# Attention and a gated feed-forward layer on one core: the normalisation is stated at the start of an attention step, and the first feed-forward units at the start of the last steps

## The chip, the cores and the metric

The kernel runs on one core of a Trainium2 chip. The metric is the device time of one execution, in microseconds (us); less is better. Before the change it is 1184.77 us, the median of 3 runs (1184.61 to 1186.2). The core has five engines, each with a queue of its own that it works through in order: TensorE (PE; its weight loads are shown apart as PEld), VectorE (DVE), ScalarE (ACT), GpSimd (POOL), and SyncE (SP), which here only issues DMA transfers.

## The reference

Attention with a forget gate over 8 batches of 8 heads, 576 positions and 64 dimensions, then a feed-forward layer (512 to 2048 to 512) over the 4608 tokens. Shapes and the handling of inputs are left out:

```python
def _attn_ref(q, k, v, f):
    scores = np.matmul(q, k.transpose(0, 1, 3, 2)) / np.sqrt(D)
    cum = np.cumsum(np.log(np.clip(f, 0.0001, 1.0)), axis=-1)
    decay = cum[:, :, :, None] - cum[:, :, None, :]
    scores = np.where(causal, -1000000000.0, scores + decay)
    attn = np.exp(scores - np.max(scores, axis=-1, keepdims=True))
    attn = attn / (np.sum(attn, axis=-1, keepdims=True) + 1e-09)
    return np.matmul(attn, v)

def _moe_ref(x, w_in, w_out):
    h = x @ w_in
    sp = np.maximum(h, 0.0) + np.log1p(np.exp(-np.abs(h)))
    return (h * erf(sp)) @ w_out
```

`causal` marks the keys behind a query. The inputs are float32, the weights float64.

## The kernel before

**Two phases.** Attention runs in 64 steps, two for each pair of heads, followed by four steps in which the last tiles drain while the feed-forward layer begins. Then the feed-forward layer runs alone. A step's tile holds some of the query blocks of both heads: an even step the blocks of 576 and 192 keys, an odd step those of 448, 320 and 64 keys (`BLOCKS`, `END`). A tile t passes through these stages, each in a step of its own as far as the loop `for t in range(NH + 5)` puts it there:

- step t: `scores(t)` on TensorE (L358, then a matmul that adds the mask, L363), into a PSUM pool `ps_s` of two buffers, one for each head, which is used again in the next step; `reduce(t, 0)` and `reduce(t, 1)` on VectorE (L379) add the decay, write the row to SBUF as `pr` and accumulate its extreme into `st`.
- step t + 1: `exps` on ScalarE (L391), for one head and then the other, with the row sums accumulated into `st`.
- step t + 2: `normalize`, which adds 1e-9 to the sums and takes their reciprocal on VectorE (L396, L397) and multiplies the rows of `pr` by it on GpSimd (L401).
- step t + 3: `transposes` on TensorE (L413) into three PSUM banks `t`, four for an odd tile, of which only three buffers exist, so that the fourth waits until the first is evacuated; `evacuate` copies the banks to SBUF as `pt`, the first two on ScalarE (L422), the others on VectorE (L420, L418).
- step t + 4: `values` on TensorE (L440), into the one buffer of `ps_o`.
- step t + 5: `store`, copies on VectorE (L449, L452, L453) to `xo`, and after an odd step a DMA to `xt_d` (L455).

**Order.** TensorE, VectorE, ScalarE and GpSimd run their instructions in the order in which the code states them. Only SP's DMAs are ordered by a scheduler. What one step states for an engine is therefore a queue: before the change VectorE has `store`, two `reduce`, `evacuate`, the reciprocal, and last a piece of `convert`.

**Weights on the side.** From step 4 to step 67 each step also has one piece of `convert`, which turns float64 weights into two float32 parts: for each of 16 loads one piece on ScalarE (L285), then one on VectorE (L289), then two instructions (L294, L296), then two (L299, L302) and one on GpSimd (L303).

**Feed-forward.** A unit (256 tokens by 256 of the 2048 features) is one `Moe.step`: `up` has 24 matmuls (L126) into a PSUM tile `ph`; ScalarE computes softplus (L132) into `e`; in groups of units the error function follows (L135), each change of function with a table load; VectorE multiplies and rounds (`gate`, L141 and L143), GpSimd takes the rest (L144), and `down` comes at least four units later (L163 to L165). A step that loads the next x also casts it on ScalarE (L111) and subtracts on GpSimd (L112). The first four units, of the first 256 tokens, are stated in steps 64 to 67. Their PSUM is that of `ps_s`, which is free after step 63. `up` of unit 0 to 3 therefore stands at the end of TensorE's part of these steps, behind `transposes` and `values`.

Of the kernel before, what the change touches and what calls it, by code (L numbers as in the profile page):

```python
# [225 lines left out]
def attention_moe(ctx, tc, q2, k2, vp, f, w_in, w_out, out):  # L226
# [32 lines left out]
    moe = Moe(tc, xt_d, out, xp, wide4)  # L259
# [51 lines left out]
    with ExitStack() as ph:  # L311
# [18 lines left out]
        def load(p):  # L330

            q = io.tile([P, PAD + S], F32, name=f"q{p}", tag="q")
            k = io.tile([P, S], F32, name=f"k{p}", tag="k")
            nc.sync.dma_start(out=q, in_=q2[p // NP, p % NP])
            nc.sync.dma_start(out=k, in_=k2[p // NP, p % NP])
            c = io.tile([P, 2, S], F32, name=f"c{p}", tag="c")
            if p:
                for j in range(2):
                    n = 2 * p + j
                    nc.sync.dma_start(out=c[:, j], in_=cum_d[n:n + 1].rearrange("a s -> (a s)").partition_broadcast(P))  # L340
            pairs[p] = [q, k, c]

        def load_values(p):

            v = wk.tile([P, 9, P], F32, name=f"v{p}", tag="v")
            nc.sync.dma_start(out=v, in_=vp[p // NP, p % NP].rearrange("p (c d) -> p c d", c=9))
            vals[p] = v

        def scores(t):


            p, half = divmod(t, 2)
            q, k = pairs[p][:2]
            s = [ps_s.tile([P, 1024], F32, name=f"s{t}_{j}", tag="s") for j in range(2)]
            for at, i, k0, k1 in PARTS[half]:
                for j in range(2):
                    h = slice(64 * j, 64 * j + 64)
                    nc.tensor.matmul(out=s[j][:, at:at + k1 - k0], lhsT=q[h, PAD + START[i]:PAD + END[i]],  # L358
                                     rhs=k[h, k0:k1], start=i > 0, stop=k1 < END[i])
            for j in range(2):  # L360
                for i in BLOCKS[half]:
                    first = max(0, START[i])
                    nc.tensor.matmul(out=s[j][:, SCOL[i] + first:SCOL[i] + END[i]], lhsT=eye,  # L363
                                     rhs=upper[:, first - START[i]:], start=False, stop=i != 3)
            raw_scores[t] = s
            probs[t] = wk.tile([P, TCOLS[half]], F32, name=f"pr{t}", tag=f"pr{half}")
            stats[t] = wk.tile([P, 3, 2, len(BLOCKS[half])], F32, name=f"st{t}", tag=f"st{half}")

        def row(t, i, j):

            return probs[t][:, TOFF[i] + j * END[i]:TOFF[i] + (j + 1) * END[i]]

        def reduce(t, j):
            p, half = divmod(t, 2)
            c, s, st = pairs[p][2], raw_scores[t][j], stats[t]
            for m, i in enumerate(BLOCKS[half]):
                to, score, decay_ = (x.rearrange("p (k n) -> p k n", n=64) for x in (
                    row(t, i, j), s[:, SCOL[i]:SCOL[i] + END[i]], c[:, j, :END[i]]))
                nc.vector.tensor_tensor_reduce(  # L379
                    out=to[:, ::-1] if j else to, in0=score, in1=decay_, scale=-0.125, scalar=BIG,  # L380
                    op0=ALU.add, op1=ALU.min, accum_out=st[:, 0, j, m:m + 1])
            if j:
                del raw_scores[t]
                if half:
                    del pairs[p]

        def exps(t, j):
            st = stats[t]
            for m, i in enumerate(BLOCKS[t % 2]):
                seg = row(t, i, j)  # L390
                nc.scalar.activation(out=seg, in_=seg, func=AF.Exp, bias=st[:, 0, j, m:m + 1], scale=-1.0,  # L391
                                     accum_out=st[:, 1, j, m:m + 1])

        def normalize(t):
            st = stats.pop(t)
            nc.vector.tensor_scalar(out=st[:, 1], in0=st[:, 1], scalar1=1e-9, scalar2=None, op0=ALU.add)  # L396
            nc.vector.reciprocal(out=st[:, 2], in_=st[:, 1])  # L397
            for m, i in enumerate(BLOCKS[t % 2]):
                for j in range(2):
                    seg = row(t, i, j)  # L400
                    nc.gpsimd.tensor_scalar(out=seg, in0=seg, scalar1=st[:, 2, j, m:m + 1], scalar2=1.0,  # L401
                                            op0=ALU.mult, op1=ALU.mult)

        def transposes(t, a):

            half = t % 2
            if a == 0:
                pts[t] = wk.tile([P, 1600 if half else 1536], F32, name=f"pt{t}", tag=f"pt{half}")
            banks[t, a] = b = ps_t.tile([P, 512], F32, name=f"t{t}_{a}", tag="t")
            for n, (i, j, *ch) in enumerate(BANKS[half][a]):  # L410

                at = TOFF[i] + (i * P if j is None else 2 * END[i] - ch[0] * P - P if j else ch[0] * P)
                nc.tensor.transpose(out=b[:, n * P:(n + 1) * P], in_=probs[t][:, at:at + P], identity=ident)  # L413

        def evacuate(t, a):
            b, pt = banks.pop((t, a)), pts[t]
            if a == 3:
                nc.vector.tensor_copy(out=pt[:, 1536:], in_=b[:, 64:128])  # L418
            elif a == 2:
                nc.vector.tensor_copy(out=pt[:, 1024:1536], in_=b)  # L420
            else:
                nc.scalar.copy(out=pt[:, 512 * a:512 * a + 512], in_=b)  # L422
            if a == len(BANKS[t % 2]) - 1:
                del probs[t]
# [18 lines left out]
        def store(t):  # L443
            p, half = divmod(t, 2)
            o = held.pop(t)
            if half == 0:
                held["x"] = xo = wk.tile([P, S], F32, name=f"xo{p}", tag="xo")
                blocks = xo[:, 64:].rearrange("p (a q) -> p a q", a=4)
                nc.vector.tensor_copy(out=blocks[:, ::3], in_=o[:, :256].rearrange("p (a q) -> p a q", a=2))  # L449
            else:  # L450
                xo = held.pop("x")
                nc.vector.tensor_copy(out=xo[:, 192:448], in_=o[:, :256])  # L452
                nc.vector.tensor_copy(out=xo[:, :64], in_=o[:, 256:320])  # L453
                b, pp = divmod(p, NP)
                nc.sync.dma_start(out=xt_d[pp * P:(pp + 1) * P, b * S:(b + 1) * S], in_=xo)  # L455
                del vals[p]

        NH = B * H
# [17 lines left out]
        for t in range(NH + 5):  # L476
            there = [0 <= t - n < NH for n in range(6)]
            p, half = divmod(t, 2)
            if half == 0 and t + 4 < NH:
                load(p + 2)  # L480
            if half == 0 and there[2]:
                load_values(p - 1)
            if there[5]:
                store(t - 5)
            if there[0]:
                scores(t)
            if there[1]:
                exps(t - 1, 0)
            if there[0]:
                reduce(t, 0)  # L490
            if there[3]:
                for a in range(3):
                    transposes(t - 3, a)
                evacuate(t - 3, 0)
            if there[3] and len(BANKS[(t - 3) % 2]) == 4:
                transposes(t - 3, 3)
            if there[4]:
                values(t - 4)
            if there[1]:
                exps(t - 1, 1)  # L500
            if there[0]:
                reduce(t, 1)
            if there[3]:
                for a in range(1, len(BANKS[(t - 3) % 2])):
                    evacuate(t - 3, a)
            if there[2]:
                normalize(t - 2)
            if t >= 4 and todo:
                convert(*todo.pop(0))
            if t == NH - 2:  # L510
                moe.load_x(0)
                moe.split_x(0)
            if t == NH - 1:
                early.close()
                moe.ep = moe_pools.enter_context(tc.tile_pool(name="ep", bufs=2, side="right"))
                moe.ps_ha = moe_pools.enter_context(tc.tile_pool(name="ps_ha", bufs=4, space=PSUM, side="right"))
            if NH <= t < NH + 4:
                moe.step()
        assert not todo and not pts and not held and not vals

    w2 = ctx.enter_context(tc.tile_pool(name="w2", bufs=1))
# [44 lines left out]
```

## Time and profile before

| | before |
|---|---|
| median of 3 runs | 1184.77 us |
| the profiled execution | 1185.39 us |
| its span, first to last instruction | 1183.6 us |
| attention, last start of scores (L358) | 342.29 us |
| start of feed-forward unit 0 (L126) | 354.42 us |
| first `down` (L163) | 377.92 us |
| mean granted TensorE clock | 0.999 |

Times in the profile count from the first instruction. In a row of the timeline the columns are start, duration, engine, line, operation, output and inputs by the program's names, and count; an idle time of the engine just before stands in brackets with what ended it. Rows of one kind that follow one another are merged. The two instructions of a matmul, its weight load (PEld) and the matmul (PE), are shown apart. A row of the chain of waits is a piece of time on the path that ended last, charged to the engine that worked in it. The profiled execution lasts 1.8 us longer than its span, for what lies around the first and the last instruction.

### The profile page before, as it was taken

What the parts mean: (1) busy time and instruction counts of PE and PEld (TensorE: products, weight loads), DVE (VectorE), ACT (ScalarE), POOL (GpSimd) and SP (SyncE); (2) the same over time, 40 slices, a digit from 0 to 9 for tenths busy, and PEclk for the clock granted to TensorE, in tenths of its full rate; (3) what the DMA queues carried; (4) which work ended last, traced back from release to release, by engine and by line L of the source; (5) the groups of instructions that cost most, each with busy time, mean ns of one, the idle gap of its engine ahead of it and who ended that gap; (6) DMA issues with size and microseconds to landing.
All of it is one profiled execution on the core that took longest, in us unless ns stands there. A gap on an engine that the chain in (4) does not pass through costs nothing.

```text
span 1183.6 us, 22838 instructions
## 1 busy us (share of the span) xinstructions
PE 1152.4 (97%) x8992; PEld 1010.0 (85%) x8992; DVE 563.4 (48%) x1473; ACT 598.9 (51%) x1231; POOL 474.1 (40%) x531
## 2 busy tenths in 40 slices
PE   5999999999999999999999999999999999999998
PEld 3777777777779999999999999998999999998987
DVE  4888888888874665665322322321231231231221
ACT  3777777777775676565423422432432342242432
POOL 1565666555673444444432432232232232232221
PEclk9999999999999999999999999999999999999999
DMA  7566767667641222421221221210110110100000
GB/s 249 187 229 230 240 215 244 213 220 239 208 145 56 79 100 75 139 73 54 89 72 54 77 85 54 71 37 1 37 36 1 36 35 2 37 15 23 18 19 18
DMA packets 56618, 118.68 MB, mean 100 GB/s; under 512 B 4672, under 2 KB 19008, under 8 KB 56512
## 3 DMA queue, kind: packets, MB, share of 16 engines
q1 hardware_dynamic: 56512, 117.23, 30.2%
q8 instruction: 71, 1.16, 0.4%
q14 instruction: 35, 0.29, 0.1%
HBM read 93.47 MB, written 23.74 MB: 99 GB/s over the span
## 4 chain that ended last, share of the span: by engine, by line
PE 82%; DVE 9%; POOL 7%; issue 1%; ACT 1%; DMA 0%; POOLq 0%; ACTq 0%
PE ph L126 35%; PE y L165 11%; PE y L163 11%; PE y L164 11%; POOL pr L401 7%; DVE pr L379 6%; PE s L358 5%; PE o L440 4%; PE t L413 3%; DVE pt L420 2%; PE s L363 1%; DVE st L397 1%; DMA fd<-in_f_dram 0%; DVE c L325 0%; DVE st L396 0%
## 5 line engine op out<-in xcount | busy, mean ns | idle before, releaser
L126 PE MATMUL ph<-xh,w 128*128 128x256 f32 x2304 | 435.8, 282 | 0.0
L126 PEld LDWEIGHTS ph<-xh,w 128*128 128x128 f32 x2304 | 367.0, 191 | 5.9
L144 POOL TENSOR_TENSOR gl<-e,gh 128x512 fp32r<-128x512 f32 x144 | 186.8, 1297 | 354.0 <-DVE gh L143 348.7
L126 PE MATMUL ph<-xl,w 128*128 128x256 f32 x1152 | 325.0, 282 | 0.0
L132 ACT ACTIVATE e<-ph 128x512 f32<-128x512 f32 x144 | 86.2, 598 | 448.3 <-PE ph L126 447.9
L401 POOL TENSOR_SCALAR pr<-pr,st 128x576 f32<-128x576 f32 (+4 forms) x320 | 179.9, 580 | 160.6 <-DVE st L397 132.7
L165 PE MATMUL y<-w,gl 128*128 128x512 f32 x576 | 228.2, 396 | 0.0
L163 PE MATMUL y<-w,gh 128*128 128x512 f32 x576 | 228.1, 396 | 0.0
L164 PE MATMUL y<-w,gh 128*128 128x512 f32 x576 | 227.2, 394 | 0.0
L126 PEld LDWEIGHTS ph<-xl,w 128*128 128x128 f32 x1152 | 219.3, 190 | 5.7
L391 ACT ACTIVATE pr<-pr,st 128x576 f32<-128x576 f32 (+3 forms) x320 | 176.5, 555 | 8.4 <-DVE st L379 8.4
L143 DVE CAST gh<-e 128x512 fp32r<-128x512 f32 x144 | 86.6, 601 | 174.6 <-PE y L164 163.0
L379 DVE CUSTOM_DVE_ANT_0 pr<-s,c 128x576 f32<-128x576 f32 (+3 forms) x320 | 136.5, 485 | 54.4 <-PE s L363 46.3
L141 DVE TENSOR_TENSOR e<-e,ph 128x512 f32<-128x512 f32 x144 | 97.9, 680 | 103.1 <-ACT e L135 101.7
L165 PEld LDWEIGHTS y<-w,gl 128*128 128x128 f32 x576 | 108.7, 189 | 25.9
L358 PE MATMUL s<-k,q 64*128 64x320 f32 (+4 forms) x768 | 114.8, 424 | 13.4 <-DMA k<-in_k_dram 8.3
L164 PEld LDWEIGHTS y<-w,gh 128*128 128x128 f32 x576 | 108.8, 189 | 20.7
L413 PE MATMUL t<-ident,pr 128*128 128x128 f32 x800 | 112.5, 281 | 14.0 <-POOL pr L401 12.9
L112 POOL TENSOR_TENSOR xl<-xr,xh 128x1024 fp32r<-128x1024 f32 x27 | 65.8, 2439 | 149.3 <-ACT xh L111 149.3
L163 PEld LDWEIGHTS y<-w,gh 128*128 128x128 f32 x576 | 108.8, 189 | 19.7
L422 ACT COPY pt<-t 128x512 f32<-128x512 f32 x128 | 73.6, 577 | 82.0 <-PE t L413 82.0
L358 PEld LDWEIGHTS s<-k,q 64*128 64x128 f32 x768 | 75.4, 194 | 43.4 <-issue 18.7
(50 smaller groups left out, 1009.3 us busy)
## 6 DMA issues: line engine op xcount, KB each, us to landing
v<-in_vp_dram SPq DMA_DIRECT2D x32, 576.0 KB, 6.1
c<-cum_d SPq DMA_DIRECT2D x62, 288.0 KB, 4.8
xr<-xt_d SPq DMA_DIRECT2D x27, 512.0 KB, 4.1
q<-in_q_dram SPq DMA_DIRECT2D x32, 320.0 KB, 2.9
k<-in_k_dram SPq DMA_DIRECT2D x32, 288.0 KB, 3.4
xt_d<-xo SPq DMA_DIRECT2D x32, 288.0 KB, 5.7
wraw<-in_w_in_dram SPq DMA_DIRECT2D x16, 512.0 KB, 5.7
wraw<-in_w_out_dram SPq DMA_DIRECT2D x16, 512.0 KB, 5.5
```

Of the source, the lines that this page charges most:

```text
L126: nc.tensor.matmul(out=ps[:, e], lhsT=w[:, kd, fs], rhs=x[:, kd], start=kd == 0 and n == 0, stop=kd == KD - 1 and n == 2)
L141: nc.vector.tensor_mul(e_, e_, h_)
L143: nc.vector.tensor_copy(out=gh, in_=e_)
L144: nc.gpsimd.tensor_tensor(out=gl, in0=e_, in1=gh.bitcast(F32), op=ALU.subtract)
L163: nc.tensor.matmul(out=y[tb], lhsT=gh[:, cs], rhs=wh[:, e], start=first, stop=False)
L164: nc.tensor.matmul(out=y[tb], lhsT=gh[:, cs], rhs=wl[:, e], start=False, stop=False)
L165: nc.tensor.matmul(out=y[tb], lhsT=gl[:, cs], rhs=wh[:, e], start=False, stop=last)
L358: nc.tensor.matmul(out=s[j][:, at:at + k1 - k0], lhsT=q[h, PAD + START[i]:PAD + END[i]], rhs=k[h, k0:k1], start=i > 0, stop=k1 < END[i])
L379: nc.vector.tensor_tensor_reduce(out=to[:, ::-1] if j else to, in0=score, in1=decay_, scale=-0.125, scalar=BIG, op0=ALU.add, op1=ALU.min, ...
L391: nc.scalar.activation(out=seg, in_=seg, func=AF.Exp, bias=st[:, 0, j, m:m + 1], scale=-1.0, accum_out=st[:, 1, j, m:m + 1])
L401: nc.gpsimd.tensor_scalar(out=seg, in0=seg, scalar1=st[:, 2, j, m:m + 1], scalar2=1.0, op0=ALU.mult, op1=ALU.mult)
L413: nc.tensor.transpose(out=b[:, n * P:(n + 1) * P], in_=probs[t][:, at:at + P], identity=ident)
```

## The change

Two statements of the step's loop are moved. `normalize(t - 2)` was stated after the evacuations of the step; it is now stated ahead of `store`, `scores` and all else but the loads. `moe.step()`, in steps 64 to 67, was stated last; it is now stated ahead of `normalize`.

```diff
                 load_values(p - 1)
+            if NH <= t < NH + 4:
+                moe.step()
+            if there[2]:
+                normalize(t - 2)
             if there[5]:
                 store(t - 5)
...
                 for a in range(1, len(BANKS[(t - 3) % 2])):
                     evacuate(t - 3, a)
-            if there[2]:
-                normalize(t - 2)
             if t >= 4 and todo:
...
                 moe.ps_ha = moe_pools.enter_context(tc.tile_pool(name="ps_ha", bufs=4, space=PSUM, side="right"))
-            if NH <= t < NH + 4:
-                moe.step()
```

No instruction of attention or of the feed-forward layer is added or removed. ScalarE's table loads are placed where the function changes, and there are two more of them.

On VectorE, between the reductions of step 62 and step 63, before the change (`pt59` is the evacuated tile of step 59, `st60` the sums of tile 60, `wraw14` a weight load, `xo29` an output tile):

```order
L420 COPY pt59_4829<-t59_2_4840 128x512
L418 COPY pt59_4829<-t59_3_4846 128x64
L396 TENSOR_SCALAR st60_4676<-st60_4676 128x4
L397 RECIPROCAL st60_4676<-st60_4676 128x4
L294 TENSOR_SCALAR wraw14_4656<-wtop14_4730 128x512
L296 SCALAR_TENSOR_TENSOR wraw14_4656<-wraw14_4656 128x512
L449 COPY xo29_4885<-o58_4848 128x2x128
```

and after it:

```order
L420 COPY pt59_4835<-t59_2_4846 128x512
L418 COPY pt59_4835<-t59_3_4852 128x64
L294 TENSOR_SCALAR wraw14_4656<-wtop14_4730 128x512
L296 SCALAR_TENSOR_TENSOR wraw14_4656<-wraw14_4656 128x512
L396 TENSOR_SCALAR st61_4757<-st61_4757 128x6
L397 RECIPROCAL st61_4757<-st61_4757 128x6
L449 COPY xo29_4893<-o58_4854 128x2x128
```

The same place in the queue now has the reciprocal of tile 61 where it had that of tile 60, and the piece of weight conversion stands ahead of it.

On ScalarE, in step 64 and the start of step 65, before the change (`t61` are the transposes of tile 61, `pr63` the last tile's rows, `e0` the softplus of unit 0):

```order
L422 COPY pt61_4978<-t61_0_4979 128x512
L391 ACTIVATE pr63_4901,st63_4902<-pr63_4901,st63_4902 128x448
L391 ACTIVATE pr63_4901,st63_4902<-pr63_4901,st63_4902 128x320
L391 ACTIVATE pr63_4901,st63_4902<-pr63_4901,st63_4902 128x64
L422 COPY pt61_4978<-t61_1_4984 128x512
L285 ACTIVATE wtop15_5024<-wraw15_4960 128x512
L132 ACT_TABLE_LOAD
L132 ACTIVATE e0_5051<-ph0_5026 128x512
L422 COPY pt62_5055<-t62_0_5056 128x512
```

and after it:

```order
L132 ACT_TABLE_LOAD
L132 ACTIVATE e0_4997<-ph0_4972 128x512
L391 ACT_TABLE_LOAD
L391 ACTIVATE pr63_4909,st63_4910<-pr63_4909,st63_4910 128x448
L391 ACTIVATE pr63_4909,st63_4910<-pr63_4909,st63_4910 128x320
L391 ACTIVATE pr63_4909,st63_4910<-pr63_4909,st63_4910 128x64
L422 COPY pt61_5011<-t61_0_5012 128x512
```

The softplus of unit 0 has moved from behind the last exponentials to ahead of all six of them, with a table load on either side, and the first evacuation of tile 61 stands behind it.

On GpSimd, the end of the normalisations, before the change (`xl1` is the lower part of the second x):

```order
L401 TENSOR_SCALAR pr62_4822<-pr62_4822,st62_4823 128x192 x2
L401 TENSOR_SCALAR pr63_4901<-pr63_4901,st63_4902 128x448 x2
L401 TENSOR_SCALAR pr63_4901<-pr63_4901,st63_4902 128x320 x2
L401 TENSOR_SCALAR pr63_4901<-pr63_4901,st63_4902 128x64 x2
L112 TENSOR_TENSOR xl1_5130<-xr1_5125,xh1_5129 128x1024
```

and after it:

```order
L401 TENSOR_SCALAR pr62_4828<-pr62_4828,st62_4829 128x192 x2
L112 TENSOR_TENSOR xl1_5083<-xr1_5078,xh1_5082 128x1024
L401 TENSOR_SCALAR pr63_4909<-pr63_4909,st63_4910 128x448 x2
L401 TENSOR_SCALAR pr63_4909<-pr63_4909,st63_4910 128x320 x2
L401 TENSOR_SCALAR pr63_4909<-pr63_4909,st63_4910 128x64 x2
```

The subtraction for the second x stands ahead of the last tile's normalisation instead of behind it. On TensorE the 24 matmuls of units 0 to 3 stand ahead of the transposes and values of steps 64 to 67 instead of behind them.

## Prediction, made before the changed kernel had run

> **What bounds the kernel now.** I read the page first, for the engines over the whole span, and then the stages one by one.
>
> ```profile
> PE 1152.4 (97%) x8992; PEld 1010.0 (85%) x8992; DVE 563.4 (48%) x1473; ACT 598.9 (51%) x1231; POOL 474.1 (40%) x531
> ```
>
> A TensorE that is busy 97% of the span seems to leave nothing. But a matmul that waits inside a group, and the tail of one under the next, are counted as busy, so I looked at two stages (each row: the stretch, its length, then the busy time of each engine).
>
> ```profile
> 150.00:200.00 50.00, 48.14 (x572) 39.28 (x571) 42.22 (x158) 37.27 (x116) 29.18 (x51) 1.00 0.70 225
> 600.00:800.00 200.00, 200.00 (x1269) 180.77 (x1268) 54.94 (x89) 71.30 (x97) 64.53 (x43) 1.00 0.20 64
> ```
>
> From about 372 us to the end TensorE does feed-forward work without a gap (200.00 of 200.00), and no line of the diff acts there after the first units: whatever time is won or lost before 372 us moves the end by as much. Attention is different. Who waited for whom between 60 and 340 us (total, times, longest):
>
> ```profile
> PEld t L413 <- POOL pr L401: 19.6, 40, 0.6
> ```
>
> The transposes wait for GpSimd's normalisation. The chain of waits shows the whole loop; one turn of it:
>
> ```profile
> 200.47 0.20 DVE st L397
> 200.86 2.68 POOL pr L401 x4
> 203.58 0.91 PE t L413 x6
> 204.49 1.47 PE o L440 x28
> 205.97 1.66 PE s L358 x12
> 207.62 0.40 PE s L363 x6
> 208.03 0.62 DVE pr L379
> ...
> 210.31 0.60 DVE pt L420
> 211.02 0.20 DVE st L397
> ```
>
> Reciprocal, normalisation, transposes, values, the next scores, their mask, the reduction of those scores, an evacuation, and the next reciprocal: 211.02 − 200.47 = 10.55 us for a pair of steps. The reciprocal is in this ring only because it stands behind the reduction on VectorE's in-order queue. Its data come from elsewhere.
>
> **What the change removes in attention.** TensorE's own rows of the same two steps give its pace without the wait:
>
> ```profile
> 200.33 1.57 PE L358 MATMUL s<-k,q 64*128 64x320 f32 x12
> 202.06 1.16 PE L413 MATMUL t<-ident,pr 128*128 128x128 f32 x7
> 203.58 0.91 PE L413 MATMUL t<-ident,pr 128*128 128x128 f32 x6 [0.36 <-POOL pr L401]
> 204.42 1.54 PE L440 MATMUL o<-pt,v 128*64 128x128 f32 x28
> 205.89 1.73 PE L358 MATMUL s<-k,q 64*128 64x448 f32 x12
> 207.85 1.51 PE L413 MATMUL t<-ident,pr 128*128 128x128 f32 x12
> 209.28 1.66 PE L440 MATMUL o<-pt,v 128*64 128x128 f32 x32
> 210.88 0.54 PE L358 MATMUL s<-k,q 64*128 64x320 f32 x2
> ```
>
> From start to start: even scores with their mask 1.73 us; values of 28 matmuls 1.47; odd scores with mask 1.96; twelve transposes that wait for nothing 1.43, or 0.119 each; values of 32 matmuls 1.60. The other thirteen transposes took 2.36 (202.06 to 204.42); at 0.119 each they would take 1.55. The sum is 1.73 + 1.55 + 1.47 + 1.96 + 1.43 + 1.60 = 9.74 us a pair. The pace over all of attention comes from the first and the last pair of this form:
>
> ```profile
> 34.47 1.19 PE L413 MATMUL t<-ident,pr 128*128 128x128 f32 x7
> 338.60 1.02 PE L413 MATMUL t<-ident,pr 128*128 128x128 f32 x7
> ```
>
> That is 29 pairs in 304.13 us, or 10.49 each. If TensorE becomes the bound, 10.49 − 9.74 = 0.75 us goes in each pair, **21.7 us** in all (the 19.6 us of waits above, over some 27 pairs, say the same).
>
> Does the wait really go? The normalisation of an odd step's tile starts at 200.86 and TensorE asks for it from 202.06. After the change its reciprocal stands at the start of that odd step instead of its end, one step of VectorE's queue earlier, some 5 us. The normalisation (2.68 us for four of its six instructions in the chain above) then ends before the transposes are due. The reciprocal must not come before the row sums, which ScalarE accumulates late in the step ahead:
>
> ```profile
> 204.91 0.19 ACT L391 ACTIVATION_READ_ACCUMULATOR pr<-pr,st 128x1 f32 x1
> 205.12 0.25 DVE L396 TENSOR_SCALAR st<-st 128x4 f32<-128x4 f32 x1
> ```
>
> The last sum of the odd tile is there at 205.10; VectorE gets to the place where its reciprocal will stand at about 205.1. So it finds it ready, or almost.
>
> **What is late next.** Scores reuse the PSUM of the step before, so they wait for its reduction (L379). The even reduction runs to 204.38, while TensorE at its own pace wants to start odd scores 4.75 us after even ones (205.08): a margin of 0.7 us. The odd one ends at 210.30 and TensorE comes at 210.88: 0.58. VectorE as a whole has 42.22 of 50 us, 8.9 a pair against 9.74. It is tight only where weights are converted, one step in two:
>
> ```profile
> 201.27 0.75 DVE L302 CAST w<-wtop 128x512 fp32r<-128x512 f32 x1
> ...
> 215.81 0.40 DVE L294 TENSOR_SCALAR wraw<-wtop 128x512 int32<-128x512 int32 x1
> 216.24 1.13 DVE L296 SCALAR_TENSOR_TENSOR wraw<-wraw 128x512 int32<-128x512 int32 x1
> ```
>
> Between two reductions VectorE then evacuates (0.8), converts (1.5), makes the reciprocal (0.4) and copies the output (0.4): 3.1 us, where TensorE leaves 0.7 + 1.96 + 0.2 = 2.9. In the next step it is 0.6 + 1.4 (the cast's 0.75 and 0.65 ahead of it) + 0.4 + 0.6 = 3.0 against 0.58 + 1.73 + 0.2 = 2.5. VectorE is late by 0.2 and 0.5 us in two of four steps; both fit into the margins of 0.7 and 0.58, so I take nothing for them. If neither margin holds, that is 0.7 us in four steps, 14.5 times: 10 us given back. The order of GpSimd's own work is the same as before until step 65, and SP's loads of q, k, c and v keep their places; a pair that is 7% shorter asks for 7% more than the 225 GB/s above, with loads two pairs ahead, so I take nothing for that either.
>
> **The last steps.** In these the feed-forward unit goes ahead of the step's transposes and values, and on ScalarE its softplus goes ahead of the last exponentials.
>
> ```profile
> 345.69 1.66 PE L440 MATMUL o<-pt,v 128*64 128x128 f32 x32
> 348.74 0.55 PE L413 MATMUL t<-ident,pr 128*128 128x128 f32 x3 [1.39 <-POOL pr L401]
> ...
> 360.38 0.38 PE L126 MATMUL ph<-xh,w 128*128 128x256 f32 x1
> ...
> 363.35 1.47 PE L413 MATMUL t<-ident,pr 128*128 128x128 f32 x12
> ...
> 372.07 0.38 PE L126 MATMUL ph<-xh,w 128*128 128x256 f32 x1
> ```
>
> A unit takes 363.35 − 360.38 = 2.97 us. Before, TensorE ends the values of step 63 at 345.69 + 1.60 = 347.29, waits for the normalisation, and starts its fourth unit at 372.07, the fifth at 375.0: 27.7 us. I lay out the same stretch after the change, in the clock of before:
>
> - Unit 0 fills the idle place: 347.29 to 350.26. Transposes of 61, three banks, to 351.7. The fourth bank needs the first to be evacuated by ScalarE, which now does softplus of unit 0 (from 350.45, 0.5), loads the exponential's table (1.28), runs three exponentials (1.54) and only then copies (0.6): 354.4. A new TensorE wait of 2.7 us. Then the last transpose and the values: 356.0.
> - Unit 1 to 359.0, transposes of 62 to 360.4, values 61 to 362.0, unit 2 to 365.0.
> - GpSimd's lower part of the next x (2.36) now stands ahead of the normalisation of 63. It waits for softplus of unit 1 and the cast of x on ScalarE (until 360.8), ends at 363.2, and the normalisation at 366.3, so the transposes of 63 wait to 366.6: 1.1 us lost. Values 62 to 368.2, unit 3 to 371.2, values 63 to 372.8, where the fifth unit starts.
>
> 375.0 − 372.8 = **2.2 us** won. The durations of the table loads and exponentials:
>
> ```profile
> 366.07 1.28 ACT L135 ACT_TABLE_LOAD   x1
> 367.37 1.16 ACT L135 ACTIVATE e<-e 128x512 f32<-128x512 f32 x2
> ```
>
> Two loads are added; the first lies in ScalarE's idle time ahead of softplus, the second is in the 2.7 us above. The Trainium skill ("ScalarE: Activation LUTs", section "What ACT_TABLE_LOAD costs") gives 1283 ns and some 1380 ns of drain with it. Here the next activation starts 1.30 us after the load does, so the trace has the load and no such drain; by the page the wait would be 1.4 us longer and the sum 0.8 us less than 2.2.
>
> **The sum.** The profiled execution took 1185.39 us, 0.62 over the median of the runs shown. 1185.39 − 21.7 − 2.2 = 1161.5; I leave 0.03 us a pair for short waits that 9.74 doesn't hold, 1 us, and less the 0.62 the median would be about **1162**.
>
> **The rivals.**
>
> - *VectorE takes over in converting steps.* For it: the margins of 0.58 to 0.7 us were read while TensorE waited, and 3.1 and 3.0 us stand against 2.9 and 2.5. Against: the conversions now stand ahead of the normalisation instead of beside it, and L296's 1.13 us can hardly get longer. It gives back up to 10 us: 1172. Chance 0.17.
> - *TensorE's clock falls at the new gap.* The last steps had a fall already:
>
> ```profile
> 348.74:354.42 5.68, 5.10 (x41) 4.22 (x41) 1.76 (x7) 4.47 (x11) 4.84 (x8) 0.70 0.96 331
> ```
>
>   The granted clock is 0.70 there, right behind the wait of 1.39 us and shorter ones. If the clock halves, a mean of 0.70 over 5.68 us is 3.4 us at half rate, which costs 1.7. My layout above is at full clock, so it holds this gain; a fall at the new 2.7 us wait would take up to 1.7 back: 1163.7. The Trainium skill ("TensorE: Matmul & The Clock Gate", section "Part 1: The HAM clock gate") lets the clock fall after an idle window of about 3.4 us, by which 2.7 us is safe; this trace fell with transposes inside the window. Chance 0.35, inside the forecast's range.
> - *Slower: the reciprocal stalls VectorE.* At the start of a step it holds the output copy and the reduction behind it until ScalarE's last exponential. It finds the sums ready with almost nothing to spare (205.10 against 205.12), but the reduction behind it cannot start before the scores end, 1.73 us after they begin, and that is its cover. It decides from 1.7 + 0.75 = 2.5 us of lateness in one step of each pair, where the whole gain is eaten. At 3 us (as long as ScalarE's two tiles of exponentials in an odd step, 2 × 1.54) the period is 9.74 + 1.3 = 11.0, and the time 1185.4 + 29 × 0.55 − 2.2 = 1199. Against: ScalarE is busy 37.27 of 50 us, and what it waits for, the transposes, comes earlier. Chance 0.04.
> - *Nothing moves*: some wait that I don't see holds 10.49, and the time is 1183 to 1185. Chance 0.04.
>
> **How the numbers follow.** The forecast, 1162 with 1157 to 1167 of its own, has 0.75 with the clock's fall in it. The lower end is TensorE's rows running 0.15 us a pair shorter than 9.74. The range reaches to the VectorE rival at 1172. Some 0.2% (2.4 us) is what a measurement here tells from no change: faster 0.93, same 0.03, slower 0.04.
>
> **What would show it.** Right: between 60 and 340 us the rows of transposes waiting for normalisation are gone or under 3 us; pairs at 9.7 to 9.8; GpSimd's normalisation ends before the transposes start; a wait of 2 to 3 us for an evacuation ahead of the last transpose of 61. Wrong: scores waiting for L379, with VectorE's reduction no longer waiting for the mask (it has taken over); or the sum's row (L396) waiting for ScalarE at each odd step.

## The result, and the profile after

| | before | changed |
|---|---|---|
| median, runs of one comparison | 1185.39 us (1184.61 to 1186.2, 4 runs) | 1165.13 us (1164.68 to 1166.43, 4 runs) |
| ratio, 95% interval | | 0.9831 [0.9814, 0.9848] |
| the profiled execution, and its span | 1185.39, 1183.6 us | 1164.68, 1162.9 us |

The engines over the whole span, then the stretch from 150 to 200 us (length, then busy time of PE, PEld, DVE, ACT and POOL), of the changed kernel:

```profile
PE 1143.0 (98%) x8992; PEld 1009.8 (87%) x8992; DVE 547.2 (47%) x1473; ACT 601.3 (52%) x1233; POOL 458.9 (39%) x531
```

```profile
150.00:200.00 50.00, 50.00 (x617) 42.05 (x615) 42.05 (x167) 40.43 (x127) 29.55 (x54) 1.00 0.76 245
```

TensorE is busy for all of the 50 us, where 48.14 stood before. The chain of waits of the changed kernel between 180 and 215 us, first its shares by line and then pieces of it (start, length, engine, operand, line, count):

```profile
by line: PE o L440 32.4%; PE s L358 31.3%; PE t L413 29.4%; PE s L363 7.1%
...
182.44 1.57 PE t L413 x13
...
192.29 1.57 PE t L413 x13
```

GpSimd and VectorE are gone from it: TensorE follows TensorE, and a pair is 192.29 − 182.44 = 9.85 us. The waits of the changed kernel between 60 and 340 us (who waits for whom: total, times, longest):

```profile
DVE pr L379 <- PE s L363: 31.2, 28, 1.6
...
PEld t L413 <- POOL pr L401: 3.6, 15, 1.1
```

The transposes' wait for the normalisation has fallen from 19.6 us to 3.6. Of these, 1.1 us are one weight load in the last steps, at 333.86, which the list puts down to the normalisation although that had ended at 330.58; it stands ahead of a transpose that waits for an evacuation (below). GpSimd normalises an odd tile from 186.76 to 189.61 us, and its transposes start at 192.13. VectorE's reductions still wait for the mask of the scores, so VectorE has not become the bound.

Where the time went is read from four rows of TensorE's timeline after the change (start, duration, engine, line, operation, count):

```profile
34.65 1.67 PE L413 MATMUL t<-ident,pr 128*128 128x128 f32 x13
...
320.45 1.73 PE L413 MATMUL t<-ident,pr 128*128 128x128 f32 x13
...
323.59 1.73 PE L358 MATMUL s<-k,q 64*128 64x448 f32 x12
...
357.21 0.39 PE L163 MATMUL y<-w,gh 128*128 128x512 f32 x1
```

| stretch | before | after | difference |
|---|---|---|---|
| start of the program to the first thirteen transposes | 34.47 | 34.65 | +0.18 |
| 29 pairs | 304.13 | 285.80 | −18.33 |
| last thirteen transposes to the last scores | 3.69 | 3.14 | −0.55 |
| last scores to the first `down` | 35.63 | 33.62 | −2.01 |

These sum to −20.71, the difference of the two profiled executions (1185.39 − 1164.68). A pair is 9.855 us on average, 10.49 before.

### The profile page after: what moved, and what is told of

It is laid out like the page before. It is cut to its first block, busy times and chain, and to the rows that moved or that the text cites. A ratio compares the mean times of both kernels' runs of the same rounds, so it can differ in the third digit from the quotient of the medians.

```text
span 1162.9 us, 22871 instructions
## 1 busy us (share of the span) xinstructions
PE 1143.0 (98%) x8992; PEld 1009.8 (87%) x8992; DVE 547.2 (47%) x1473; ACT 601.3 (52%) x1233; POOL 458.9 (39%) x531
## 4 chain that ended last, share of the span: by engine, by line
PE 97%; DVE 1%; ACT 1%; POOL 0%; DMA 0%; issue 0%; POOLq 0%
PE ph L126 35%; PE y L165 12%; PE y L163 12%; PE y L164 12%; PE s L358 9%; PE o L440 8%; PE t L413 8%; PE s L363 2%; DVE pr L379 0%; POOL pr L401 0%; DMA fd<-in_f_dram 0%; DVE c L325 0%; DVE pt L420 0%; ACT fd L321 0%; DVE cum L325 0%
## 5 line engine op out<-in xcount | busy, mean ns | idle before, releaser
L401 POOL TENSOR_SCALAR pr<-pr,st 128x576 f32<-128x576 f32 (+4 forms) x320 | 164.5, 535 | 119.7 <-DVE st L397 93.8
L112 POOL TENSOR_TENSOR xl<-xr,xh 128x1024 fp32r<-128x1024 f32 x27 | 65.6, 2430 | 157.9 <-ACT xh L111 157.9
L413 PE MATMUL t<-ident,pr 128*128 128x128 f32 x800 | 104.0, 275 | 2.6 <-DVE pt L420 1.8
```

## The experiments

Times are medians of four to ten runs, but of two for the normalisation behind the conversion; each ratio is to runs of the kernel before on the same chip. "Pair" is the mean of the 29 pairs, "stretch" the time from the last scores to the first `down`, each read from the same four rows as above. Where an expectation counts to the start of the fifth unit, that is the stretch less the 2.97 us of one unit.

| | us (range) | ratio [95%] | pair | stretch |
|---|---|---|---|---|
| changed | 1165.13 (1164.68 to 1166.43) | 0.9831 [0.9814, 0.9848] | 9.855 | 33.62 |
| changed, repeated | 1164.97 (1164.9 to 1165.19) | 0.9833 [0.9819, 0.9846] | 9.852 | 33.64 |
| normalisation alone | 1163.61 (1163.54 to 1163.64) | 0.9824 [0.9809, 0.9838] | 9.855 | 32.29 |
| normalisation alone, repeated | 1163.48 (1162.92 to 1163.57) | 0.9819 [0.9806, 0.9832] | 9.857 | 32.29 |
| units alone | 1183.96 (1182.29 to 1185.34) | 0.9994 [0.9984, 1.0003] | 10.505 | 35.36 |
| normalisation ahead of the evacuations | 1173.45 (1171.89 to 1173.83) | 0.9904 [0.9889, 0.9919] | 10.099 | 35.33 |
| normalisation behind the conversion | 1215.43 (1214.21 to 1216.65) | 1.0252 [1.0232, 1.0273] | 11.428 | 36.69 |
| fourth bank behind the values | 1164.46 (1163.58 to 1165.67) | 0.9834 [0.9817, 0.985] | 9.853 | 34.10 |
| normalisation ahead of the unit | 1164.11 (1163.93 to 1164.24) | 0.9819 [0.9804, 0.9834] | 9.858 | 32.62 |
| exponentials ahead of unit 0 | 1164.44 (1164.08 to 1164.62) | 0.9822 [0.9806, 0.9839] | 9.852 | 33.06 |
| unit 2 inside tile 63 | 1165.24 (1163.82 to 1166.15) | 0.9828 [0.9813, 0.9842] | 9.855 | 33.31 |
| single bank first | 1160.52 (1160.42 to 1162.21) | 0.9798 [0.9785, 0.9812] | 9.704 | 33.66 |
| the same, but for tiles 61 and 63 | 1159.02 (1158.38 to 1159.21) | 0.9785 [0.9771, 0.9798] | 9.704 | 32.47 |

### The two halves apart

The first kernel moves the normalisation and leaves the units last:

```diff
+            if there[2]:
+                normalize(t - 2)
             if there[5]:
                 store(t - 5)
...
-            if there[2]:
-                normalize(t - 2)
```

> The normalisation is stated first, the feed-forward units stay last in steps 64 to 67. Theory A, each part of the change brings its own share (18.3 us in attention, 2.05 us in the last steps): pairs at 9.85 us as after the change, the stretch from the last scores to the fifth unit back at 32.7 us, time 1165.1 + 2.05 = 1167.2. Theory B, the early normalisation alone closes the idle place at the end of attention, and the units ahead only put ScalarE's softplus and two table loads in the way: pairs at 9.85, the stretch at 28.9 to 29.9 us instead of 30.65, time 1163.4 to 1164.4. The clock does not fall under either if no gap above 1 us is left.

The second moves the units and leaves the normalisation:

```diff
+            if NH <= t < NH + 4:
+                moe.step()
             if there[5]:
                 store(t - 5)
...
-            if NH <= t < NH + 4:
-                moe.step()
```

> The units are stated first, the normalisation stays last. Both theories: attention as before (pairs at 10.49 us). Theory A: the stretch from the last scores to the fifth unit 30.65 us instead of 32.7, time 1185.4 - 2.05 = 1183.3. Theory B: the same or more is won here, because unit 0 fills the place in which TensorE waited for the late normalisation and in which its clock fell (1.7 us): stretch 30.4 to 31, no slice of granted clock under 1.0, time 1183 to 1184. If the two parts together are worth less than the sum of each alone, they overlap.

The normalisation alone is not a part of the gain, it is more than all of it: 1163.61 us, 1.5 under the whole change, with the same pairs. TensorE's timeline of the normalisation alone, in the last steps (in brackets the idle time ahead and what ended it):

```profile
323.77 1.73 PE L358 MATMUL s<-k,q 64*128 64x448 f32 x12
...
330.07 1.09 PE L413 MATMUL t<-ident,pr 128*128 128x128 f32 x6 [0.34 <-POOL pr L401]
...
343.86 0.30 PE L413 MATMUL t<-ident,pr 128*128 128x128 f32 x1 [0.89 <-ACT pt L422]
...
356.06 0.39 PE L163 MATMUL y<-w,gh 128*128 128x512 f32 x1
```

From 323.77 to 356.06 are 32.29 us, 3.34 less than before and 1.33 less than with the units first. TensorE waits 0.34 + 0.89 = 1.23 us here. The same rows of the changed kernel, with the evacuations on VectorE and ScalarE around the first of them:

```profile
332.36 1.28 ACT L391 ACT_TABLE_LOAD   x1
333.05 0.69 DVE L420 COPY pt<-t 128x512 f32<-128x512 f32 x1 [2.21 <-PE t L413]
333.65 0.67 ACT L391 ACTIVATE pr<-pr,st 128x448 f32<-128x448 f32 x1
...
333.89 0.30 PE L413 MATMUL t<-ident,pr 128*128 128x128 f32 x1 [0.88 <-DVE pt L420]
...
335.20 0.56 ACT L422 COPY pt<-t 128x512 f32<-128x512 f32 x1
```

```profile
344.53 1.09 PE L413 MATMUL t<-ident,pr 128*128 128x128 f32 x7
346.25 0.77 PE L413 MATMUL t<-ident,pr 128*128 128x128 f32 x5 [0.63 <-POOL pr L401]
...
347.89 0.30 PE L413 MATMUL t<-ident,pr 128*128 128x128 f32 x1 [0.88 <-DVE pt L420]
```

It waits three times, 0.88 + 0.63 + 0.88 = 2.39 us: 1.16 more than the normalisation alone, most of the 1.33. From a tile's first transpose to its values, tile 63 takes 3.59 us (344.53 to 348.12) against 2.59 with the normalisation alone (341.50 to 344.09), and tile 61 takes 2.58 (331.54 to 334.12) against 2.34 (328.75 to 331.09). So 1.0 of the 1.33 us lies in tile 63, whose normalisation now stands behind GpSimd's subtraction for the second x, and 0.24 in tile 61. With the normalisation alone, tile 61's transposes pause for the normalisation, and ScalarE copies the first bank in that pause (330.15 to 330.72); with the units first, twelve run without a pause and the thirteenth waits for VectorE's copy.

The units alone bring nothing that can be measured (0.9994, the interval holds 1). Their stretch is 0.27 us shorter than before, and in it the clock falls. TensorE's timeline, and a window around it (after the busy times the granted clock):

```profile
364.27 0.76 PE L413 MATMUL t<-ident,pr 128*128 128x128 f32 x5 [0.53 <-POOL pr L401]
365.90 0.30 PE L413 MATMUL t<-ident,pr 128*128 128x128 f32 x1 [0.88 <-DVE pt L420]
366.13 2.76 PE L440 MATMUL o<-pt,v 128*64 128x128 f32 x28
```

```profile
364.00:369.00 5.00, 3.86 (x35) 3.42 (x36) 3.03 (x7) 1.39 (x3) 2.35 (x5) 0.72 0.30 110
```

The 28 matmuls of the values take 2.76 us instead of 1.54, at a mean granted clock of 0.72.

Both sides were then run again on one chip, to see whether 1.5 us is more than the spread:

> The normalisation-only kernel beside the changed kernel on one chip. If the units stated first cost time as the stretch of the last steps shows (29.3 against 30.65 us), it is 1.3 us below the changed kernel: 1163.6. If that difference was one of runs, the two are equal.

> The changed kernel itself, for the comparison with the two others on one chip: 1165.1.

The ranges don't meet (1162.92 to 1163.57 against 1164.9 to 1165.19). The stretches repeat as well (32.29 against 33.64). The second statement of the change costs 1.5 us when the first is there.

### What the early reciprocal has to pass

From the kernel before, the normalisation is stated only a little earlier, behind the second reduction and ahead of the evacuations:

```diff
             if there[0]:
                 reduce(t, 1)
+            if there[2]:
+                normalize(t - 2)
             if there[3]:
                 for a in range(1, len(BANKS[(t - 3) % 2])):
```

> From the kernel before, the normalisation is stated behind the second reduction of its step and ahead of the evacuations: still behind the reduction, but 0.6 to 0.8 us earlier. Theory 1, only the 0.75 us by which it is late in a pair counts: pairs at 9.85 to 9.95 us, time 1166 to 1170. Theory 2, the reciprocal has to leave the ring through the reduction altogether: pairs at 10.3 or more, time above 1179.

A pair is 10.10 us: 0.39 of the 0.63 us, for a reciprocal that has passed one or two copies. Neither theory had that size. The chain shows why; the ends of one turn of it, and the waits between 60 and 320 us:

```profile
194.46 2.88 POOL pr L401 x4
197.38 0.91 PE t L413 x6
...
204.61 1.70 POOL pr L401 x2
```

```profile
PEld t L413 <- POOL pr L401: 10.0, 28, 0.8
```

The ring is still there in this turn, which is 204.61 − 194.46 = 10.15 us: the 10.55 of before less the evacuation's 0.60, which it no longer holds, and plus 0.20, since the normalisation's first four instructions take 2.88 us instead of 2.68, now beside VectorE's copies and conversion. In other turns between 130 and 300 us the chain stays on TensorE, so this ring no longer sets every pair. The tile's wait is halved (10.0 us of 19.6), not gone. The last steps gain only 0.3 us (35.33 against 35.63), and as before the granted clock falls in them, to 0.50 from 340 to 342 us.

The other way, the normalisation is stated behind the conversion:

```diff
-            if there[2]:
-                normalize(t - 2)
             if t >= 4 and todo:
                 convert(*todo.pop(0))
+            if there[2]:
+                normalize(t - 2)
```

> From the kernel before, the normalisation is stated behind the piece of weight conversion instead of ahead of it: later by that piece (none, 0.65, 1.5 or 1.4 us in four steps). Theory 1, the reciprocal's place in VectorE's queue sets the pace through the ring: in odd steps the pieces of 0.65 and 1.4 us enter the ring, 1.0 us a pair on average, pairs at 11.5 us, time 1185 + 29 = 1214; more, up to 1230, if the even steps' 1.5 us are not covered either. Theory 2, the gain in attention came from GpSimd and VectorE no longer running conversion and normalisation side by side: conversion is ahead of the normalisation here too, so pairs stay at 10.5 or fall, time 1185 or less.

```profile
190.36 0.60 DVE pt L420
190.96 0.61 DVE wtop L299
...
191.60 0.43 DVE w L302
...
192.11 0.29 POOL w L303
...
193.35 2.27 POOL pr L401 x4
```

The chain now holds the conversion's pieces between the evacuation and the normalisation, L299 and L302 on VectorE and behind them L303 on GpSimd, the pair takes 11.43 us and the kernel 1215.4. So the wait grows and shrinks with what stands ahead of the reciprocal in VectorE's queue; in this kernel a part of it, 1.24 us in this turn (192.11 to 193.35), is L303, which now stands ahead of the normalisation on GpSimd. That the normalisation no longer ran beside the conversion was a second candidate for the gain; here it does not run beside it either (its first four instructions take 2.27 us instead of 2.68), and the kernel is slower. Running side by side lengthened the ring of before by up to 0.4 us; it is not what closes it.

### The thirteen transposes

After the change thirteen transposes take 1.66 us, not 1.55. The changed kernel's timeline, TensorE with its weight loads and ScalarE:

```profile
192.13 1.73 PE L413 MATMUL t<-ident,pr 128*128 128x128 f32 x13
192.82 0.59 ACT L422 COPY pt<-t 128x512 f32<-128x512 f32 x1 [0.94 <-PE t L413]
193.53 0.14 PEld L413 LDWEIGHTS t<-ident,pr 128*128 128x128 f32 x1 [0.16 <-issue]
193.79 1.54 PE L440 MATMUL o<-pt,v 128*64 128x128 f32 x28
```

The thirteenth is alone in its bank, for which there is no fourth buffer: it starts at 193.53, right behind the copy of the first bank (192.82 + 0.59 = 193.41). That the copy is what it waits for is read from these times; the trace names no releaser for the wait of 0.16 us. The first try moves it away from the copy, behind the values:

```diff
-            if there[3] and len(BANKS[(t - 3) % 2]) == 4:
-                transposes(t - 3, 3)
             if there[4]:
                 values(t - 4)
+            if there[3] and len(BANKS[(t - 3) % 2]) == 4:
+                transposes(t - 3, 3)
```

> From the changed kernel, the transpose of an odd tile's fourth bank is stated behind the values of the tile before instead of ahead of them. Theory 1, the 0.11 us a pair between 9.74 and 9.85 are the fourth bank's wait for the evacuation of the first: pairs at 9.74, time 1165.1 - 3.3 - up to 1.5 in the last steps = 1160.3 to 1161.8. Theory 2, the pace of thirteen transposes in a row is simply lower: pairs at 9.85, time 1165. A loss, above 1166, would say that VectorE waits for the late bank.

```profile
309.13 1.48 PE L413 MATMUL t<-ident,pr 128*128 128x128 f32 x12
310.54 1.54 PE L440 MATMUL o<-pt,v 128*64 128x128 f32 x28
312.01 0.33 PE L413 MATMUL t<-ident,pr 128*128 128x128 f32 x1
312.27 1.73 PE L358 MATMUL s<-k,q 64*128 64x448 f32 x12
```

It gains nothing (pairs of 9.853). Twelve take 1.41 us now, 0.1175 each, but the lone one takes 0.26 between the values and the scores: 309.13 to 312.27 is 3.14 us, against 1.66 + 1.47 = 3.13 in the changed kernel. A lone transpose between other matmuls pays as much as it had waited.

The second try, from the normalisation alone, states the single bank first and has ScalarE evacuate it at once, so that no bank of this tile comes behind a full-size copy:

```diff
+            if there[3] and len(BANKS[(t - 3) % 2]) == 4:
+                transposes(t - 3, 3)
+                evacuate(t - 3, 3)
             if there[3]:
                 for a in range(3):
                     transposes(t - 3, a)
...
-            if there[3] and len(BANKS[(t - 3) % 2]) == 4:
-                transposes(t - 3, 3)
...
-                nc.vector.tensor_copy(out=pt[:, 1536:], in_=b[:, 64:128])
+                nc.scalar.copy(out=pt[:, 1536:], in_=b[:, 64:128])
```

> From the normalisation-only kernel, an odd tile's bank with one transpose is stated first instead of fourth, and ScalarE evacuates it at once (64 columns) where VectorE did it late. The last bank then needs a buffer that is free early. Theory 1, the thirteen transposes take 1.66 us instead of 13 x 0.119 = 1.55 because the fourth bank waits for an evacuation: pairs at 9.74 to 9.76, and the 0.89 us wait of tile 63 goes, time 1163.6 - 3.0 - 0.9 = 1159.7. Theory 2, the extra 0.11 us belongs to a lone transpose wherever it stands (0.26 us when it stood behind the values): pairs at 9.85, time 1162.7 to 1163.6.

```profile
199.85 1.59 PE L413 MATMUL t<-ident,pr 128*128 128x128 f32 x13
201.37 1.31 PE L440 MATMUL o<-pt,v 128*64 128x128 f32 x20
...
326.52 1.64 PE L413 MATMUL t<-ident,pr 128*128 128x128 f32 x13 [2.18 <-POOL pr L401]
...
340.39 0.66 PE L413 MATMUL t<-ident,pr 128*128 128x128 f32 x4 [0.75 <-ACT pt L418]
```

The thirteen take 1.52 us (199.85 to 201.37) and the pair 9.704, 0.15 less. In the last steps it loses: the single bank needs the block that is normalised last, so all of tile 61 waits 2.18 us for it. Tiles 61 and 63 were therefore put back to the old order:

```diff
-            if there[3] and len(BANKS[(t - 3) % 2]) == 4:
+            if there[3] and len(BANKS[(t - 3) % 2]) == 4 and t - 3 < 61:
                 transposes(t - 3, 3)
                 evacuate(t - 3, 3)
...
+                if t - 3 >= 61 and len(BANKS[(t - 3) % 2]) == 4:
+                    transposes(t - 3, 3)
```

> As in e10_single_bank_first, but the tiles 61 and 63 keep the old order, with the fourth bank last and VectorE evacuating it. If the 1.4 us that e10's stretch from the last scores to the first down was longer than e1's came from these two tiles alone (the wait of 2.18 us for the block normalised last, and the evacuation that ScalarE has more), the stretch is 32.3 us as in e1 (e10 33.66), the pairs stay at 9.70 us, and the time is 1160.5 - 1.4 = 1159.1 us. If the stretch is longer for another reason, such as tile 61's and 63's neighbours coming earlier than the feed-forward's x, it stays at 33.7 and the time at 1160.5.

The stretch is 32.47 us (319.08 to 351.55), and the time, 1159.02 us, is the best of all: 25.5 us under its runs of before (1184.52), 6 under the change.

### The order inside the last steps

Three kernels look for the 1.33 us. In the first, from the change, the two moved statements are swapped:

```diff
+            if there[2]:
+                normalize(t - 2)
             if NH <= t < NH + 4:
                 moe.step()
-            if there[2]:
-                normalize(t - 2)
```

> From the changed kernel, the normalisation is stated ahead of the unit in steps 64 and 65 (the two moved statements are swapped), so GpSimd normalises the last tile before it subtracts for the second x. If the 0.63 us wait of tile 63's transposes comes from that subtraction, it goes: stretch from the last scores to the fifth unit 30.0 instead of 30.65 us, time 1164.5. If tile 63 is late through ScalarE's late exponentials instead, the wait stays: 1165.1.

The stretch is 32.62 us: 1.0 of the 1.33 is back, all of what tile 63 had lost (its transposes to its values take 2.58 us, 344.98 to 347.56). The wait of 0.63 us for tile 63's normalisation is gone, because GpSimd's subtraction of the second x (L112) no longer stands ahead of it. The two waits of 0.88 us stay.

In the second, from the change, the last exponentials are stated ahead of unit 0:

```diff
             if NH <= t < NH + 4:
+                if t == NH:
+                    exps(t - 1, 0)
+                    exps(t - 1, 1)
                 moe.step()
```

> From the changed kernel, in step 64 all six last exponentials are stated ahead of the unit; ScalarE then needs no return to the exponential's table (two loads fewer). If the units-first order costs its 1.25 us through ScalarE's queue (softplus and table loads ahead of the exponentials), stretch 29.4 to 30.0 us, time 1163.9 to 1164.5. If it costs through the fourth bank, whose 0.88 us wait for an evacuation no longer lies beside other work, that wait stays at 0.88 twice and the stretch stays at 30.0 to 30.6, time 1164.5 to 1165.1.

The stretch is 33.06 us, 0.56 shorter; to the fifth unit that is 30.09, just over the border of 30.0 between the two expectations. ScalarE's copies of tile 61 come earlier, yet TensorE's wait ahead of the last transpose of 61 stays at 0.88 us: ScalarE was not what it waited for. The gain lies in tile 63, whose wait for the normalisation falls from 0.63 to 0.23 us, since GpSimd's subtraction starts at 340.34 instead of 341.28. Two table loads fewer had been expected, but their number stays: the weight conversion (L285) now has one more of its own, and ScalarE has 1233 instructions as in the changed kernel.

In the third, from the normalisation alone, unit 2 is put between the third and the fourth bank of tile 63, into the wait of 0.89 us:

```diff
                 evacuate(t - 3, 0)
+            if t == NH + 2:
+                moe.step()
             if there[3] and len(BANKS[(t - 3) % 2]) == 4:
                 transposes(t - 3, 3)
```

> From the normalisation-only kernel, unit 2 is stated between the third and the fourth bank of tile 63. If the 0.89 us wait of that fourth bank is for the evacuation of an earlier bank, the unit covers it: stretch 28.5 us instead of 29.4, time 1163.6 - 0.9 = 1162.7. If the unit's evacuations and gate only push the wait behind it, time 1163.6 or more.

```profile
349.66 1.66 PE L440 MATMUL o<-pt,v 128*64 128x128 f32 x32 [2.21 <-DVE xo L449]
```

The wait is covered, and another takes its place: the last values wait 2.21 us for VectorE to copy out the only `ps_o` buffer (L449). The stretch is a microsecond longer than without the edit.

## Why the prediction came out as it did

1162 us was forecast and 1165.13 came.

**The removed wait: mechanism right.** The reciprocal's place in VectorE's queue was what closed the ring, and with it a step earlier TensorE follows TensorE, and the normalisation ends before the transposes start. The row of waits is at 3.6 us rather than under 3, and 1.1 of it is the one wait in the last steps that was for an evacuation. Moving it alone gives the same pairs, and moving it by less or the other way gives 10.10 and 11.43 us.

**The pair: one term too small.** 9.74 us was forecast, 9.855 came. The terms of the changed kernel's pair from 192.13 us on are 1.66, 1.47, 1.95, 1.44, 1.59 and 1.73, of which five are within 0.01 of the forecast. The thirteen transposes were taken at 13 × 0.119 = 1.55, the pace of twelve, and take 1.66: the fourth bank waits for a buffer, which the description of the kernel before had said. While the wait for the normalisation was there it had hidden this one. The 29 pairs gave 18.33 us where 21.7 was forecast, and these 3.4 us are the main difference. Less the 1 us set aside for short waits and the 0.55 us won in the last pair, and with the 0.2 us lost at the start and the 0.2 missing in the last steps, 2.2 us are left between the 1162.5 that the sum gives for a profiled execution and 1164.68. With the single bank first these thirteen take 1.52, as the sum had it.

**The last steps: the sum close by luck, its parts not right.** 2.2 us was forecast, 2.01 came. But the forecast put the gain down to the unit that fills the wait ahead of tile 61. TensorE's other waits in the last steps of the kernel before, beside the 1.39 us:

```profile
349.51 0.66 PE L413 MATMUL t<-ident,pr 128*128 128x128 f32 x4 [0.23 <-POOL pr L401]
350.53 1.47 PE L413 MATMUL t<-ident,pr 128*128 128x128 f32 x6 [0.35 <-POOL pr L401]
...
365.71 0.30 PE L413 MATMUL t<-ident,pr 128*128 128x128 f32 x1 [0.89 <-ACT pt L422]
```

The normalisation alone, with the units last, shortens the stretch by 3.34 us: these waits fall from 2.86 us to 0.34 + 0.89, which is 1.63 less, and the clock's fall, worth an estimated 1.7 in the prediction, is gone too. The units first then cost 1.33. The step that failed is "a new TensorE wait of 2.7 us" for ScalarE: the wait was 0.88, for VectorE's copy that ends at 333.05 + 0.69 = 333.74, while ScalarE's copy of the first bank started only at 335.20, behind the transpose. So the fourth bank of this tile did not take the first bank's buffer, as the description of the kernel before has it for every odd tile; it waited for the third bank's.

The lateness of tile 63 behind GpSimd's subtraction was forecast at 1.1 us, and 1.0 comes back when the two statements are swapped. But the forecast's end of 372.8 doesn't hold it: thirteen transposes of 1.55 us from 365.0 on end at 366.55 without any wait, and the layout has 366.6. Nor does it hold the 0.88 us of tile 63's fourth bank. One wait put 1.8 us too long stands against two left out, 1.9 us together; that they cancel is luck.

The exponentials' table load took the 1.28 us forecast, and the exponential starts 1.29 us after the load (332.36, 333.65). The Trainium skill ("ScalarE: Activation LUTs", section "What ACT_TABLE_LOAD costs") has some 1380 ns of drain with it; this trace again has none behind it. With such a drain 0.8 us of the 2.2 forecast would have been left.

**VectorE takes over: no.** Its reductions still wait for TensorE. The argument against the rival was that L296 could hardly get longer; it got shorter. The groups of before from 100 to 340 us, then of the change from 100 to 320 us (total, then mean ns):

```profile
L296 DVE SCALAR_TENSOR_TENSOR wraw<-wraw 128x512 int32<-128x512 int32 x11 | 12.4, 1126 | 0.4
L302 DVE CAST w<-wtop 128x512 fp32r<-128x512 f32 x11 | 8.3, 755 | 0.4
```

```profile
L296 DVE SCALAR_TENSOR_TENSOR wraw<-wraw 128x512 int32<-128x512 int32 x11 | 7.6, 694 | 0.4
L302 DVE CAST w<-wtop 128x512 fp32r<-128x512 f32 x11 | 4.7, 427 | 0.4
```

With 0.43 and 0.33 us less, the prediction's 3.1 and 3.0 us between reductions become about 2.7 each, against 2.9 and 2.5; the 0.2 us by which the second is still over fits into its margin of 0.58.

**The clock falls at the new gap: not here.** The changed kernel around its last wait:

```profile
347.00:350.00 3.00, 2.12 (x33) 1.95 (x33) 2.43 (x5) 0.51 (x2) 1.00 (x1) 1.00 0.15 58
```

The granted clock is 1.00. With the units alone it fell to 0.72 around two waits of 0.53 and 0.88 us, hardly different from these. In the traces here the granted clock falls to 0.50 in the last steps of all four kernels with the normalisation stated late (before, units alone, ahead of the evacuations, behind the conversion), and in none of the ten executions with it at the start of the step, although two of those have a wait of 2.18 and of 2.21 us. Before the change it fell at 350.7, when TensorE had had only waits and transposes since 347.29; the changed kernel has 3.59 us of these (344.53 to 348.12) and no fall. The Trainium skill ("TensorE: Matmul & The Clock Gate", section "Part 1: The HAM clock gate") names an idle window of about 3.4 us; the falls with transposes inside the window don't agree with that read as unbroken idleness. What decided between the kernels stays open.

**The slower rival and no change: no.** VectorE finds the sums nearly always ready at the reciprocal's new place, and the one long wait there, 2.88 us in step 65, had no scores behind it.

## What to carry to other kernels

Where an engine works its queue in order, look in the chain of waits for a short instruction that stands behind work it doesn't need, and try it a whole stage earlier: here 0.4 us of reciprocal cost 0.63 us of every 10.5, and half the way gave only part of it. When a wait is removed, count the next one from the buffers, not only from the rows, since the old wait hides it. And test each statement of a change alone: one of these two was worth more than both together, and the other, beside it, cost 1.5 us.

## What the runs showed of the hardware beside it

VectorE's L296 and L302 take 1126 and 755 ns beside GpSimd's normalisation and 694 and 427 without it, and in the kernel with the normalisation behind the conversion L302 takes 0.43 too. L289 and L299 have 0.65 to 0.68 us before and after; in the kernel with the normalisation ahead of the evacuations, where they run wholly beside it, they take 0.89 and 0.87. GpSimd is slower as well: its 128x448 instruction takes 794 ns before and 638 in the changed kernel. Which resource they share was not tried.

The start of the program differs by some 1.5 us between kernels in which nothing before 60 us of TensorE's order has changed that would explain it. The same twelve matmuls, of the changed kernel and of the units alone:

```profile
26.13 4.10 PE L358 MATMUL s<-k,q 64*128 64x448 f32 x12 [1.01 <-DVE st L379]
```

```profile
26.06 2.65 PE L358 MATMUL s<-k,q 64*128 64x448 f32 x12 [1.02 <-DVE st L379]
```

4.10 us against 2.65. In the kernel before, which has the same order as the units alone up to step 64, they take 4.04. With the normalisation alone they take 4.17, in a stretch where the granted clock reads 0.50; but in the changed kernel it reads 1.00 there, so the granted clock on record does not explain the difference, and the cause stays open. Differences of 1 to 2 us between single executions are therefore read from the stretches, not from the whole span.
